# Attention and token mixer on one core: the first chunk's scores in place of dummy products, and three other moves

## The chip, the core and the metric

The kernel runs on one core of one Trainium2 chip. A core has engines that run side by side and wait for each other through semaphores: TensorE (PE in the profile, with PEld for its weight loads), VectorE (DVE), ScalarE (ACT), GpSimd (POOL) and the queue that issues transfers (SP). The metric is device time in microseconds (us): 832.36 us is the median of three runs of the kernel before (831.63 to 832.51).

## The reference

Routed attention over 4 batches, 8 heads, 768 positions and 64 dimensions, and a token and channel mixer on its output. All is float32.

```python
q_assign = argmax(q_n . c_n);  k_assign = argmax(k_n . c_n)      # 16 clusters for each head
mask   = q_assign[:, None] == k_assign[None, :]
scores = where(mask, q @ k.T / 8, -1e9)
x      = softmax(scores) @ v                                      # then (B, S, H*D) = (4, 768, 512)
h = relu(x^T @ w_tok1) @ w_tok2;   u   = x + h^T                  # token mixing
h2 = relu(u @ w_ch1) @ w_ch2;      out = u + h2                   # channel mixing
```

## The kernel before, where the change and the steps touch it

Two heads make a pair, and there are 16 pairs. Of a pair, the scores of a half of its queries (`qh`, 384 of them) against a chunk `j` of 128 keys are a tile `sc`. It is the sum of two products: one-hot cluster vectors (`ohT`, bf16; its query part carries the factor -2^33, and a key's vector holds ones at the clusters that are not its own), which adds the mask, and q and k themselves (`T`, f32). A pair has two halves of six chunks each.

```python
def scores(g, qh, beside=None):
    for j in range(NJ):                                  # NJ = 6
        if (g, qh, j) == (0, 0, 2):
            second_first()                               # one-hots of the 2nd half: turned on PE, put by DVE, counted on ACT
        sc = ps_sc.tile([P, 2, 512], F32, tag="sc", name="sc")      # 3 buffers in PSUM
        for src, start in ((st["ohT"], True), (st["T"], False)):
            for h in range(2):
                nc.tensor.matmul(sc[:, h, 0:HS], lhsT=src[rows, 1, j], rhs=src[rows, 0, js], start=start, stop=not start)
        ex = st["ex", qh, j] = work.tile([P, 2, HS], F32, name="ex")  # 9 buffers
        nc.scalar.activation(out=ex, in_=sc[:, :, 0:HS], func=ACT.Exp, scale=SM_SCALE)

def add_up(g, qh):                                       # DVE: five additions make the denominators' sums
    for j in range(1, NJ):
        nc.vector.tensor_tensor(out=acc, in0=acc if j > 1 else st["ex", qh, 0], in1=st["ex", qh, j], op=ALU.add)
```

The first pair has no earlier work to hide behind. Its beginning is written out:

```python
    keep_warm(11)                                        # dummy products of zeros
    scs = [ps_sc.tile([P, 2, 512], F32, tag="sc", name="pt") for _ in range(2)]
    tq = turn_first(0, 0, scs[0][:, 0, 0:HS])            # q of the first half turned on PE; k likewise
    ...
    keep_warm(2)
    pr = ps_sc.tile([P, 2, 512], F32, tag="sc", name="pr")
    route_products(0, pr[:, 0, 0 : HS // 2], js[0])      # similarities to the clusters, first half
    ...
    route(0, js[0])                                      # DVE: turn, maximum, one-hots
    keep_warm(3)
    route_turn_first(0)                                  # PE turns the one-hots, ACT and DVE put them into ohT
    route_products(0, pr[:, 1, 0 : HS // 2], js[1])      # second half
    route(0, js[1])
```

The loop over pairs, with what the steps need:

```python
for g in range(NPAIR):
    for qh in range(2):
        scores(g, qh, ...)
        if g == 0 and qh == 0:
            turn(1); load(2)                             # DVE turns q and k of pair 1
        if (g, qh) == (0, 1):
            route_products(1, ...); route_on(1)          # DVE: one-hots of pair 1, then a transfer that turns them
        add_up(g, qh)
    ...
    turn(g + 2); load(g + 3)
    ...
    for qh in range(2): values(g, qh)
    pair_sums(g, ...); route_products(g + 2, ...)        # both into one tile "small"
```

Token and channel mixing use Strassen's scheme in Winograd's form: seven block products (`p1 p5 c11 u2 c12 c22 c21`) and sums of blocks, `S1..S4` on the left and `T1..T4` on the right, which DVE makes. PSUM banks X, Y and Z carry the products, three buffers of X and of Z. After each product, DVE adds the bank to the result, and `between()` puts one waiting step into the stream.

```python
order = "p1 0 p1 1 p1 2 p5 0 p5 1 p5 2 c11 0 c11 1 u2 0 u2 1 u2 2 c12 0 c12 1 "
order += "c22 0 c22 1 c22 2 c12 2 c11 2 c21 0 c21 1 c21 2"
for m in ...:
    product(banks[tag, i], a, r, i, name in FIRST)       # PE
    add(x, banks[tag, i], x)                             # DVE, reads the bank
    if m in after: after[m]()
    between()                                            # late step first, then one of `others`

# second token mixing: two sums of u after product 13 (c22 0)
tok2_chunks(b, {13: lambda: (next(usums), next(usums))})

# channel mixing, first part of the first batch: the last two products of ch1 come late
def late_(i):
    product(X[i], "A22", "T4", i, False)
    nc.scalar.activation(out=a12[:, i], in_=X[i], func=ACT.Relu)
    if i == 0: sub(h2["S2"], h2["S1"], a11)
    else: sum_3(); sum_4()
late.extend([lambda: late_(0), lambda: late_(1)])
# ... and ch2_chunks starts: its p1 0, p1 1, p1 2 take the X buffers in turn
```

Of the kernel before, what the change touches and what calls it, by code (L numbers as in the profile page):

```python
# [8 lines left out]
F32 = mybir.dt.float32  # L9
BF16 = mybir.dt.bfloat16  # L10
# [7 lines left out]
B, H, S, D = 4, 8, 768, 64  # L18
C = 16
P = 128  # L20
# [30 lines left out]
def kernel(  # L51
# [320 lines left out]
    def turn_first(n, a, out):  # L372

        st = state[0]
        for j in range(HJ):
            nc.tensor.transpose(
                out=out[:, j * P : (j + 1) * P],
                in_=st["rows"][n][:, a, j].rearrange("p h d -> p (h d)"), identity=ident,
            )
        js = slice(HJ * n, HJ * n + HJ)  # L380
        return st["T"][:, a, js].rearrange("p j t -> p (j t)"), out

    def route_turn_first(n):

        for a in (1, 0):
            po = ps_av.tile([P, HJ, P], BF16, tag="av", name="po")
            for j in range(HJ):
                nc.tensor.transpose(out=po[:, j], in_=ohs[0][:, a, HJ * n + j], identity=identb)
            out = state[0]["ohT"][:, a, HJ * n : HJ * n + HJ]
            if a == 0:  # L390
                nc.vector.tensor_scalar_mul(out=out, in0=po, scalar1=-BIG)
            elif n == 0:
                nc.scalar.copy(out=out, in_=po)
            else:
                nc.vector.tensor_copy(out=out, in_=po)
# [9 lines left out]
        state[0].pop("rows")  # L405


    def scores(g, qh, beside=None):

        st = state[g]  # L410
        js = slice(HJ * qh, HJ * qh + HJ)
        for j in range(NJ):
            if (g, qh, j) == (0, 0, 2):
                second_first()
            sc = ps_sc.tile([P, 2, 512], F32, tag="sc", name="sc")
            for src, start in ((st["ohT"], True), (st["T"], False)):
                for h in range(2):
                    rows = slice(h * D, (h + 1) * D)
                    nc.tensor.matmul(  # L419
                        sc[:, h, 0:HS], lhsT=src[rows, 1, j], rhs=src[rows, 0, js],  # L420
                        start=start, stop=not start,
                    )
            if qh * NJ + j == EX and beside:
                beside()
            ex = st["ex", qh, j] = work.tile([P, 2, HS], F32, name="ex")
            nc.scalar.activation(out=ex, in_=sc[:, :, 0:HS], func=ACT.Exp, scale=SM_SCALE)  # L426

    def add_up(g, qh):
        st = state[g]
        if qh == 0:  # L430
            st["sum"] = sums.tile([P, 2, 2, HS], F32, name="sum", bufs=1)
        acc = st["sum"][:, qh]
        for j in range(1, NJ):
            nc.vector.tensor_tensor(  # L434
                out=acc, in0=acc if j > 1 else st["ex", qh, 0], in1=st["ex", qh, j], op=ALU.add
            )
# [335 lines left out]
    def ch1_pair(part, sets, beside):  # L772
# [131 lines left out]
        if sets:  # L904
            set_x("X", "Y", "p1", a12[:, 0, n0])
            sum_1()

            def late_1():
                set_x("X", None, "u2", a12[:, 0, n1])
                set_z("X", ptile("Z", HS // 2), a12)  # L910
                sub(h2["S2"], h2["S1"], a11)

            def late_2():
                set_x("X", None, "c22", a12[:, 1].rearrange("p (k t) -> p k t", k=2))
                relu(a12)
                sum_3()
                sum_4()

            late.extend([late_1, late_2])
        else:  # L920
            sum_1()
# [4 lines that stand above are left out]
                if i == 0:  # L926
                    sub(h2["S2"], h2["S1"], a11)
                else:
                    sum_3()
                    sum_4()  # L930

            late.extend([lambda: late_(0), lambda: late_(1)])

    def ch2_chunks(b, part, last, after=()):

# [57 lines left out]
    def begin():  # L993
        cen = rsmall.tile([P, D], F32, name="cen")
        nc.sync.dma_start(cen, centroids.rearrange("h c d -> (h c) d"))
        load_first()

        nc.vector.memset(ones, 1.0)
        warm = rsmall.tile([P, WMAX], BF16, name="warm")
        nc.vector.memset(warm, 0.0)  # L1000
        nc.vector.memset(cnd, 0.0)
        nc.scalar.activation(out=rsmall.tile([P, QP], F32, name="expd"), in_=ones, func=ACT.Exp)
        make_identity(nc, ident)
        nc.gpsimd.tensor_copy(out=identb, in_=ident)
        for oh in ohs:
            nc.gpsimd.memset(oh, 0.0)
        load(1)
        load_v(0)
        pw = ps_av.tile([P, HS], F32, tag="av", name="av")

        def keep_warm(n):
            for _ in range(n):
                nc.tensor.matmul(pw, lhsT=warm[:, 0:P], rhs=warm[:, P : P + HS], start=True, stop=True)

        js = [slice(0, HJ), slice(HJ, NJ)]
        keep_warm(11)
        scs = [ps_sc.tile([P, 2, 512], F32, tag="sc", name="pt") for _ in range(2)]
        tq = turn_first(0, 0, scs[0][:, 0, 0:HS])
        nc.scalar.copy(out=tq[0], in_=tq[1])
        pc = centroids_norm(cen)  # L1020
        centroids_out(pc)
        tk = turn_first(0, 1, scs[1][:, 0, 0:HS])
        nc.vector.tensor_copy(out=tk[0], in_=tk[1])
        nc.scalar.copy(out=cnT, in_=pc)
        keep_warm(2)
        pr = ps_sc.tile([P, 2, 512], F32, tag="sc", name="pr")
        route_products(0, pr[:, 0, 0 : HS // 2], js[0])
        pt = ps_sc.tile([P, 2, 512], F32, tag="sc", name="pt")
        for out, src in [turn_first(1, a, pt[:, a, 0:HS]) for a in (0, 1)]:
            nc.scalar.copy(out=out, in_=src)  # L1030
        route(0, js[0])
        keep_warm(3)
        route_turn_first(0)
        route_products(0, pr[:, 1, 0 : HS // 2], js[1])
        route(0, js[1])

    begin()
# [1 line left out]
    def route_on(g):  # L1039
        route(g)  # L1040
        route_big(g)
        route_turn(g)
# [6 lines left out]
    for g in range(NPAIR):  # L1049
        for qh in range(2):  # L1050
            scores(g, qh, g and (lambda: pair_put(g - 1)))
            if g == 0 and qh == 0:
                turn(1)
                load(2)
            if (g, qh) == (0, 1):
                route_products(1, ps_av.tile([P, HS], F32, tag="av", name="pr"))
                route_on(1)
            add_up(g, qh)
        for other in (1, 2) if g == 1 else (g + 1,) if 2 <= g < NPAIR - 1 else ():
            route_count(other)  # L1060
        if g + 2 < NPAIR:
            turn(g + 2)
        if g + 3 < NPAIR:
            load(g + 3)
        if g > 0:
            pair_out(g - 1)
        rounding(1)
        if g == NPAIR - 2:
            assert not weights
            routing.close()  # L1070
            W["ch2"] = pool("wc2pool", 1, side="right").tile([P, NCT, DM], F32, name="wc2")
            weights = list(weight_steps(stage, W, ("ch2",), 2, nc.vector))
            rounding(1)
        rounding(g == NPAIR - 1)
        for qh in range(2):
            values(g, qh)
        if g + 2 < NPAIR:
            load_v(g + 2)
        pair_turn(g)
        two = ps_sc.tile([P, 2, 512], F32, tag="sc", name="small")  # L1080
        pair_sums(g, two[:, 0, 0:HS])
        if g + 2 < NPAIR:
            route_products(g + 2, two[:, 1, 0:HS])
        pair_denominators(g)
        if g + 2 < NPAIR:
            route_on(g + 2)
        pair_reciprocals(g)
        rounding(2 if g == NPAIR - 2 else g == NPAIR - 1 or g % 2 == 0 and 0 < g < EARLY)
# [8 lines left out]
    for b in (0, 2):  # L1097
# [26 lines left out]
        if b == 2:  # L1124
            take(turning, len(turning))
            usums = u_sums()
            tok2_chunks(b, {13: lambda: (next(usums), next(usums))})
        else:
            left_weights()
            others += left_sums(0)  # L1130
            tok2_chunks(b)
            nc.sync.dma_start(spill, xs[1])
            turning = list(u_steps(0))
# [7 lines left out]
    for n, b in enumerate(batches):  # L1141
        turning = []
        for part in range(3):
            first, last = n == 0 and part == 0, n == B - 1 and part == 2
            if part == 2 and not last:
                turning = list(u_steps(batches[n + 1]))
            if first:
                others += [lambda: next(usums)] * 2
                for steps in (right_weights(0), set_left_sums(1)):
                    others += steps  # L1150
# [242 lines left out]
```

## Time and profile before

| | value |
|---|---|
| median time | 832.36 us |
| span of the profiled run | 830.0 us |
| PE busy | 818.9 us (99%) |
| DVE busy | 606.2 us (73%) |
| ACT busy | 381.3 us (46%) |
| POOL busy | 30.7 us (4%) |
| granted clock | 0.999 of full |

A row of the timeline gives the start of a group of like instructions, how long it lasted, engine, line, operation, tiles and count; what stands in brackets is the engine's idle time just before and who ended it. A float32 product shows as two records. The ends of matmuls are modelled in the profile, and so the start of the next is the better measure of what one took.

### The profile page before, as it was taken

The numbers are of one execution on the slowest core, as the hardware profiler recorded it, in microseconds if no ns is written. First come the engines' busy times: TensorE is split into PE (matmuls) and PEld (weight loads), VectorE is DVE, ScalarE is ACT, GpSimd is POOL, SyncE is SP. The second block draws the span as 40 slices with busy tenths as digits, with TensorE's granted clock in tenths as the row PEclk, the third lists the DMA queues.
The fourth block names the chain that finished last, engine by engine and source line by source line (L and its number), as shares of the span: only waits on it lengthen the run. The fifth ranks groups of instructions, "written<-read, shape, count | busy, mean of one in ns | idle before, by whom it ended". The sixth has DMA issues, their size and how long they took to land.

```text
span 830.0 us, 11458 instructions
## 1 busy us (share of the span) xinstructions
PE 818.9 (99%) x4285; PEld 525.7 (63%) x4285; DVE 606.2 (73%) x1124; ACT 381.3 (46%) x562; POOL 30.7 (4%) x28
## 2 busy tenths in 40 slices
PE   9999999999999999999999999999999999999997
PEld 4444444444444444444578787878878788787876
DVE  6879898989898878859676677655667456764654
ACT  5678777787878775145202253121541204511120
POOL 1001010101101000000000000000000000000000
PEclk9999999999999999999999999999999999999999
DMA  9886676867776334143000115000130001400002
GB/s 154 154 152 146 122 140 123 166 137 151 138 155 136 83 96 130 41 156 48 0 1 1 19 38 173 1 0 9 37 109 1 1 1 28 124 1 0 1 2 80
DMA packets 184256, 63.39 MB, mean 76 GB/s; under 512 B 172800, under 2 KB 176896, under 8 KB 183936
## 3 DMA queue, kind: packets, MB, share of 16 engines
q1 hardware_dynamic: 182592, 62.18, 34.8%
q8 instruction: 35, 0.57, 0.3%
q10 hardware_dynamic: 1600, 0.39, 0.2%
q14 instruction: 29, 0.24, 0.1%
HBM read 36.21 MB, written 7.86 MB: 53 GB/s over the span
## 4 chain that ended last, share of the span: by engine, by line
PE 90%; DVE 7%; issue 1%; ACT 0%; DMA 0%; SPq 0%; DVEq 0%; ACTq 0%
PE sc L419 18%; PE pX L940 14%; PE av L444 13%; PE pX L788 11%; PE pZ L940 7%; PE ph L523 5%; PE pY L801 4%; PE pY L940 4%; PE pZ L788 3%; PE pZ L801 3%; PE pX L762 2%; PE pX L801 2%; PE small L480 1%; DVE x L554 1%; DVE sum L434 1%; PE pZ L762 1%
## 5 line engine op out<-in xcount | busy, mean ns | idle before, releaser
L426 ACT ACTIVATE ex<-sc 128x768 f32<-128x768 f32 x192 | 151.0, 812 | 29.1 <-PE sc L419 16.9
L419 PE MATMUL sc<-qkT 64*128 64x384 f32 x768 | 155.1, 482 | 0.0
L434 DVE TENSOR_TENSOR sum<-sum,ex 128x768 f32<-128x768 f32 x128 | 127.8, 999 | 26.9 <-ACT ex L426 14.2
L444 PE MATMUL av<-ex,va 128*64 128x384 f32 x768 | 127.4, 488 | 0.0
L554 DVE TENSOR_TENSOR x<-pX,x 128x256 f32<-128x256 f32 (+1 forms) x168 | 76.1, 460 | 41.3 <-PE pX L940 40.7
L444 PEld LDWEIGHTS av<-ex,va 128*64 128x64 f32 x768 | 53.7, 137 | 71.8 <-issue 67.0
L419 PEld LDWEIGHTS sc<-qkT 64*128 64x128 f32 x768 | 67.9, 187 | 38.4 <-issue 38.3
L828 ACT COPY hA<-pX 128x384 f32<-128x384 f32 x24 | 11.5, 479 | 146.2 <-PE pX L788 146.2
L554 DVE TENSOR_TENSOR hA<-pY,hA 128x192 f32<-128x192 f32 (+1 forms) x90 | 36.8, 409 | 50.8 <-PE pY L801 36.0
L810 ACT ACTIVATE hA<-hA 128x768 f32<-128x768 f32 x35 | 29.6, 845 | 87.1 <-DVE hA L554 87.1
L788 PE MATMUL pX<-uT,wc 128*128 128x384 f32 x192 | 68.0, 487 | 0.5 <-DVE x L554 0.5
L419 PE MATMUL sc<-ohT 64*128 64x384 bf16 x384 | 62.8, 323 | 0.1
L788 PEld LDWEIGHTS pX<-uT,wc 128*128 128x128 f32 x192 | 35.7, 190 | 18.3 <-issue 1.3
L451 ACT COPY avrows<-av 128x768 uint16<-128x768 uint16 x32 | 25.5, 796 | 45.0 <-PE av L444 45.0
L554 DVE TENSOR_TENSOR x<-pZ,x 128x256 f32<-128x256 f32 (+1 forms) x84 | 36.5, 458 | 11.9 <-PE pZ L940 11.8
L523 PE MATMUL ph<-x,wt 128*128 128x512 f32 x96 | 41.6, 593 | 0.0
L419 PEld LDWEIGHTS <-ohT 64*128 64x128 bf16 x384 | 18.6, 94 | 34.3 <-issue 9.4
L940 PE MATMUL pX<-wc,hA 128*128 128x256 f32 x144 | 37.2, 381 | 1.6 <-ACT hA L925 1.2
L697 ACT COPY uT<-ucols 128x768 uint16<-128x768 uint16 x32 | 33.2, 1051 | 4.2 <-DMA ucols<-urows 4.2
L940 PE MATMUL pY<-wc,hA 128*128 128x256 f32 x144 | 35.1, 379 | 0.0
L940 PE MATMUL pZ<-wc,hS 128*128 128x256 f32 x144 | 35.0, 379 | 0.0
L788 PE MATMUL pX<-uTs,w1s 128*128 128x384 f32 x96 | 34.9, 486 | 0.0
(178 smaller groups left out, 1266.8 us busy)
## 6 DMA issues: line engine op xcount, KB each, us to landing
raw<-in_moe_w_ch_dram SPq DMA_DIRECT2D x24, 512.0 KB, 4.5
va<-in_v_dram SPq DMA_DIRECT2D x16, 384.0 KB, 3.6
out_dram<-x SPq DMA_DIRECT2D x24, 256.0 KB, 2.6
qk<-in_k_dram SPq DMA_DIRECT2D x60, 96.0 KB, 3.9
qk<-in_q_dram SPq DMA_DIRECT2D x60, 96.0 KB, 3.6
raw<-in_moe_w_tok_dram SPq DMA_DIRECT2D x3, 512.0 KB, 4.3
raw<-in_moe_w_tok_dram SPq DMA_DIRECT2D x4, 384.0 KB, 3.8
spill<-x SPq DMA_DIRECT2D x1, 1536.0 KB, 5.1
```

What stands on the lines that cost most here:

```text
L419: nc.tensor.matmul(sc[:, h, 0:HS], lhsT=src[rows, 1, j], rhs=src[rows, 0, js], start=start, stop=not start,)
L426: nc.scalar.activation(out=ex, in_=sc[:, :, 0:HS], func=ACT.Exp, scale=SM_SCALE)
L434: nc.vector.tensor_tensor(out=acc, in0=acc if j > 1 else st["ex", qh, 0], in1=st["ex", qh, j], op=ALU.add)
L444: nc.tensor.matmul(av[h * D : (h + 1) * D], lhsT=st["va"][:, h, j], rhs=ex[:, h], start=(j == 0), stop=(j == NJ - 1),)
L451: nc.scalar.copy(out=st["rows"][:, qh], in_=av.bitcast(U16).rearrange("p (t w) -> p w t", w=2))
L523: nc.tensor.matmul(pf, lhsT=W["tok1"][:, j, t * P : (t + 1) * P], rhs=xs[b][:, j], start=(j == 0), stop=(j == NJ - 1),)
L554: nc.vector.tensor_tensor(out=dst, in0=a, in1=b, op=ALU.add)
L697: nc.scalar.copy(out=out, in_=pools.pop(("ucols", i)).rearrange("p w j t -> p w (j t)"))
L788: nc.tensor.matmul(psum, lhsT=A[a][:, k, c], rhs=R[r][:, k], start=start and k == 0, stop=k == 1, skip_group_check=not start,)
L801: nc.tensor.matmul(psum, lhsT=left[which][a][:, part * P : part * P + P], rhs=right[which][r], start=start, stop=True, skip_group_check=no ...
L810: nc.scalar.activation(out=x, in_=x, func=ACT.Relu)
L940: nc.tensor.matmul(psum, lhsT=h2[a][:, k, i * P : (i + 1) * P], rhs=Bw[w][:, part + 3 * k], start=start and k == 0, stop=k == 1, skip_grou ...
```

## The change

It has four moves. None changes what is computed.

1. The q and k product of the first chunk of the first pair is issued before the one-hots are turned, in the place of three dummy products. Its tile waits open for the one-hot product. For this the buffers of the beginning are dealt out anew: q and k of the first half are turned in one tile, `pr` moves to the other PSUM pool, and one of the turned one-hots moves to the pool of the scores.
2. The turning of the second half's one-hots goes from before the third chunk to before the fourth, and the fourth chunk's product of q and k goes ahead of its one-hot product.
3. Of the first pair's second five additions, two go ahead of the routing of pair 1 on DVE.
4. Of the sums of u, the second goes from after product 13 of the second token mixing to after its last addition; and the first of the two late products of ch1 is issued at once instead of after `p1 0` of ch2.

```diff
-    def route_turn_first(n):
+    def route_turn_first(n, pq=None):
         for a in (1, 0):
-            po = ps_av.tile([P, HJ, P], BF16, tag="av", name="po")
+            po = pq if a == 0 and pq is not None else ps_av.tile([P, HJ, P], BF16, tag="av", name="po")
...
+    def score(g, sc, qh, j, name, start):
+        src = state[g][name]
+        for h in range(2):
+            rows = slice(h * D, (h + 1) * D)
+            nc.tensor.matmul(
+                sc[:, h, 0:HS], lhsT=src[rows, 1, j], rhs=src[rows, 0, HJ * qh : HJ * qh + HJ],
+                start=start, stop=not start,
+            )
+
     def scores(g, qh, beside=None):
         for j in range(NJ):
-            if (g, qh, j) == (0, 0, 2):
+            names = ["ohT", "T"]
+            if (g, qh, j) == (0, 0, HJ):
                 second_first()
-            sc = ps_sc.tile([P, 2, 512], F32, tag="sc", name="sc")
-            ... (the two products, ohT and then T)
+                names.reverse()
+            sc = st.pop("early", None)
+            if sc is None:
+                sc = ps_sc.tile([P, 2, 512], F32, tag="sc", name="sc")
+                score(g, sc, qh, j, names[0], True)
+                score(g, sc, qh, j, names[1], False)
+            else:
+                score(g, sc, qh, j, "ohT", False)
...
-    def add_up(g, qh):
+    def add_up(g, qh, js=range(1, NJ)):
...
-            late.extend([lambda: late_(0), lambda: late_(1)])
+            late_(0)
+            late.append(lambda: late_(1))
...
-        scs = [ps_sc.tile([P, 2, 512], F32, tag="sc", name="pt") for _ in range(2)]
-        tq = turn_first(0, 0, scs[0][:, 0, 0:HS])
+        turned = ps_sc.tile([P, 2, 512], F32, tag="sc", name="pt")
+        tq = turn_first(0, 0, turned[:, 0, 0:HS])
...
-        pr = ps_sc.tile([P, 2, 512], F32, tag="sc", name="pr")
-        route_products(0, pr[:, 0, 0 : HS // 2], js[0])
+        pr = ps_av.tile([P, 2, HS // 2], F32, tag="av", name="pr")
+        route_products(0, pr[:, 0], js[0])
...
-        keep_warm(3)
-        route_turn_first(0)
-        route_products(0, pr[:, 1, 0 : HS // 2], js[1])
+        pq = ps_sc.tile([P, HJ, P], BF16, tag="sc", name="po")
+        sc = state[0]["early"] = ps_sc.tile([P, 2, 512], F32, tag="sc", name="sc")
+        score(0, sc, 0, 0, "T", True)
+        route_turn_first(0, pq)
+        route_products(0, pr[:, 1], js[1])
...
             if (g, qh) == (0, 1):
                 route_products(1, ps_av.tile([P, HS], F32, tag="av", name="pr"))
+                add_up(0, 1, range(1, 3))
                 route_on(1)
-            add_up(g, qh)
+                add_up(0, 1, range(3, NJ))
+            else:
+                add_up(g, qh)
...
-            tok2_chunks(b, {13: lambda: (next(usums), next(usums))})
+            tok2_chunks(b, {13: lambda: next(usums)})
...
             if first:
+                next(usums)
                 others += [lambda: next(usums)] * 2
```

More of the change, by code (lines that the diff above doesn't have):

```diff
@@ L405, in second_first @@
         state[0].pop("rows")
+    def score(g, sc, qh, j, name, start):
[6 more added lines that the diff above has]
+            )
     def scores(g, qh, beside=None):
         st = state[g]
-        js = slice(HJ * qh, HJ * qh + HJ)
         for j in range(NJ):
-            if (g, qh, j) == (0, 0, 2):
+            names = ["ohT", "T"]
+            if (g, qh, j) == (0, 0, HJ):
                 second_first()
-            sc = ps_sc.tile([P, 2, 512], F32, tag="sc", name="sc")
[L416 to L422, printed above, removed]
+                names.reverse()
[6 more added lines that the diff above has]
+                score(g, sc, qh, j, "ohT", False)
             if qh * NJ + j == EX and beside:
@@ L426, in scores @@
             nc.scalar.activation(out=ex, in_=sc[:, :, 0:HS], func=ACT.Exp, scale=SM_SCALE)
-    def add_up(g, qh):
+    def add_up(g, qh, js=range(1, NJ)):
         st = state[g]
-        if qh == 0:
+        if "sum" not in st:
             st["sum"] = sums.tile([P, 2, 2, HS], F32, name="sum", bufs=1)
         acc = st["sum"][:, qh]
-        for j in range(1, NJ):
+        for j in js:
             nc.vector.tensor_tensor(
@@ L1021, in begin @@
         centroids_out(pc)
-        tk = turn_first(0, 1, scs[1][:, 0, 0:HS])
+        tk = turn_first(0, 1, turned[:, 1, 0:HS])
         nc.vector.tensor_copy(out=tk[0], in_=tk[1])
```

## The prediction

> **What bounds the kernel now.** I read the page first, its busy times and its chain.
>
> ```profile
> PE 818.9 (99%) x4285; PEld 525.7 (63%) x4285; DVE 606.2 (73%) x1124; ACT 381.3 (46%) x562; POOL 30.7 (4%) x28
> ...
> PE 90%; DVE 7%; issue 1%; ACT 0%; DMA 0%; SPq 0%; DVEq 0%; ACTq 0%
> ```
>
> PE is at work 99% of the span and makes 90% of the chain. So a change can win only by taking PE work away or by closing one of the few gaps on PE. The view of waits, for PE alone, lists those gaps:
>
> ```profile
> PE pX L940 <- ACT hA L925: 1.2, 2, 0.6
> PE pr L304 <- DVE qkT L1023: 0.6, 1, 0.6
> PE pX L788 <- DVE x L554: 0.5, 1, 0.5
> PE small L304 <- DVE qkT L294: 0.5, 1, 0.5
> ```
>
> Columns: total us, times, longest. These are short, since a wait counts only from the modelled end of the matmul before; measured from start to start the gaps are larger. Three of the four lines stand where the change acts, the second (the products of the first routing) does not. I then read the timeline at these places.
>
> The beginning:
>
> ```profile
> 7.84 0.65 PE L1013 MATMUL av<-warm 128*128 128x384 bf16 x3
> ...
> 8.45 0.51 PE L388 MATMUL po<-identb,oh 128*128 128x128 bf16 x6
> ```
>
> PE fills the time until the one-hots come (8.45) with three dummies, and no other PE work lies there; the first score product follows at 9.41. The end of the first pair:
>
> ```profile
> 27.86 1.83 DVE L294 STREAM_TRANSPOSE qkT<-qk 128x768 f32<-128x768 f32 x2
> ...
> 29.75 0.85 PE L304 MATMUL small<-qkT,cnd 128*32 128x384 f32 x8 [0.47 <-DVE qkT L294]
> ```
>
> PE waits for DVE to turn pair 2, so this point is set by DVE's queue and not by PE's. The end of the second token mixing:
>
> ```profile
> 389.30 0.95 DVE L551 TENSOR_TENSOR uTs<-uT 128x768 f32<-128x768 f32 x1
> ...
> 390.36 0.96 DVE L551 TENSOR_TENSOR uTs<-uT,uTs 128x768 f32<-128x768 f32 x1
> ...
> 393.63 1.88 DVE L554 TENSOR_TENSOR x<-pX,x 128x512 f32<-128x512 f32 x3
> ...
> 394.45 2.82 PE L788 MATMUL pX<-uT,wc 128*128 128x384 f32 x8 [0.50 <-DVE x L554]
> ```
>
> Two sums of u stand in DVE's queue ahead of additions that free X banks; PE's next product takes a bank only at 394.45. The first part of the channel mixing:
>
> ```profile
> 410.87 1.45 PE L788 MATMUL pX<-uTs,wc 128*128 128x384 f32 x4
> ...
> 412.36 0.49 ACT L925 ACTIVATE hA<-pX 128x384 f32<-128x384 f32 x1 [0.72 <-PE pX L788]
> ...
> 412.90 1.13 PE L940 MATMUL pX<-wc,hA 128*128 128x256 f32 x4 [0.58 <-ACT hA L925]
> ```
>
> Each late product is followed at once by a ch2 product whose X buffer is the late product's own: PE stands until ACT has read it, here and again at 415.91.
>
> **What the Trainium skill says.** "Perfetto Trace Analysis", section "Identifying the Most-Contended Engine", says that matmul busy time is a poor measure of how near PE is to its limit, because matmuls overlap. The trace agrees: a 128x512 record lasts 592 ns on average, but follows the one before after 0.43 us (six from 386.71 to 389.29). I therefore count from start to start. "PSUM — Partial Sum Buffer", section "Engine vs sequencer instructions", says that the queues of VectorE and ScalarE are strictly first in, first out, and that matmuls start and finish in program order. The trace agrees where it matters: at 393.63 DVE adds the last c21 banks after both sums of u, though u is needed later. So the order of the program is the order of the wait. "TensorEngine Tiling (Array Packing)", section "Key Properties", says that a change of the tiling mode drains TensorE. The trace shows about 0.10 us at such a place: q and k products of 64 rows repeat every 0.32 us, and the last of them before a turn (128 rows) takes 0.42.
>
> **The change part by part.**
>
> *Beginning, PE.* One chunk's q and k product is four records, two and two side by side, 2 x 0.32 = 0.64 us; the three dummies are 3 x 0.16 = 0.49, and after them PE waited 0.12. The early product starts at 7.84 and needs only what was ready at 6.5. With the 0.10 for the switch of mode, the turns start at 7.84 + 0.64 + 0.10 = 8.57 instead of 8.45: 0.12 later, and so are ohT and the first one-hot product (9.53 for 9.41). From there PE has one q and k product less, 0.64. Twelve chunks later PE is 0.64 - 0.12 = 0.52 us ahead. Moving the second turn behind the third chunk adds no work.
>
> *First pair, DVE.* Only part of this reaches the end. The first Exp can begin 0.52 earlier (9.93 for 10.45), but three now run before the counts, 9.93 + 3 x 0.81 = 12.36, and the two counts take 0.78 as before: 13.14 for 12.74. DVE's turn of pair 1 waits for them: 13.35 for 12.95, 0.40 later. Five additions follow (5.17 from 14.71 to 19.88), now until 20.28. Then the two moved additions (2.08) fill the 0.80 in which DVE waited for the routing products: until 22.36. Routing takes 2.06 (20.68 to 22.74): 24.42. Three additions of 1.04: 27.5, where it was 27.86. So pair 2 is turned 0.36 earlier and PE's product comes at 29.4 instead of 29.75. The stage wins 0.35 us, not 0.52. The turning transfer of pair 1's one-hots starts 1.5 us later and takes some 3.9 to land (28.3), ahead of the scores at 30.2.
>
> *Do the pairs after it keep this?* From pair to pair the scores begin 19.11 us apart, with almost nothing idle on PE, and where DVE holds PE once (0.27 us near 166) DVE itself was started by PE at 145.36. All of it shifts along.
>
> *Second token mixing.* With one sum of u less, c22's other additions start at 390.18, and those up to the first of c21 follow each 0.60: the bank for ch1 is free at about 393.25. PE's 16 records from 386.71 on end at 386.71 + 16 x 0.43 = 393.59. So ch1 starts at 393.59 and not 394.45: 0.86. The first record after the stand took 0.08 more, which goes too. 0.94 us. The moved sum then runs from 394.4 to 395.4; its product comes about 5 us later.
>
> *Late product.* Order now: late 0 at 410.01 (1.29), p1 0 (0.86), late 1 (1.29), p1 1 (0.86), p1 2 (0.86). Late 0's bank is read by ACT by 412.13 (after its relu of a22, until 411.64); p1 1 wants it at 413.45. Late 1's bank is read by about 414.2; p1 2 wants it at 414.31. No stand is left. p5 starts at 415.17 instead of 416.87: 1.70 us, which is two gaps of 0.74 and twice 0.10 for the first record after them. DVE has S2, S3, S4 bunched before the p1 additions, about 1.4 us behind PE; the first bank that waits for such an addition comes back five products (4.3 us) later.
>
> Sum: 0.35 + 0.94 + 1.70 = 2.99 us, and 832.36 - 2.99 = 829.4.
>
> **The rivals.** (1) DVE's new order takes the wait elsewhere: the bunched sums hold u2 or the next ch1 bank, and part of the 1.70 comes back. For it: DVE was within 0.2 us of PE in this stretch. Against it: from 421 on DVE waits 0.17 us for each product, so it catches up. If it came true, about 830.5. (2) The beginning wins nothing or loses: the early product delays the one-hots (0.12) and the counts hold DVE back more than I reckon. For it: DVE sets the end of this stage. That makes 829.8, and up to 830.2 with a loss. (3) The p1 2 bank is missed by a few hundredths, or a stand appears after the shift of other phases; 829.7. (4) All small gains vanish in a later wait: against it, the chain is PE's to the end; then 832.
>
> **Range and chances.** The repeat spread of the kernel before is 0.9 us in all. Rivals 1 to 3 all lie above my number, so the range is longer upwards: 828.5 to 831.0. Two per cent would be 16.6 us, more than all the idle time of PE: faster by over 2% 0.005, within 2% 0.985, slower 0.01.
>
> **What would show it.** In the changed profile: no wait of L940 for the late relu; the first ch1 product of the first batch about 0.9 closer to the last c21; the product of pair 2 (L304) near 29.4 and still waiting for DVE; the first scores at 9.53. PE's busy time should fall little, its gaps by some 2.5 us. I am wrong if a new wait for DVE's additions (L554) stands in ch2's first part, if that L304 comes later than 29.75, or if pairs stop being 19.11 apart.

## The result and the profile after

The changed kernel takes 829.12 us (median of 6 runs, 828.57 to 829.63). The kernel before, run beside it, takes 832.18 us (831.63 to 832.51). The ratio is 0.9965, with a 95% interval of 0.9952 to 0.9977. The span of the profiled run is 827.5 us, where it was 830.0.

The page of the changed kernel, its busy times and its chain:

```profile
PE 818.1 (99%) x4282; PEld 526.0 (64%) x4282; DVE 605.3 (73%) x1124; ACT 381.6 (46%) x562; POOL 30.6 (4%) x28
...
PE 95%; DVE 4%; ACT 0%; issue 0%; ACTq 0%; DVEq 0%
```

PE has 0.8 us less work, DVE's share of the chain has gone from 7% to 4%, and the span has 2.5 us less. So most of the gain comes from gaps and not from work. Which gaps, the view of waits of PE tells (total us, times, longest):

```profile
PE pX L952 <- ACT hA L897: 0.4, 1, 0.4
PE pt L376 <- ACT qkT L1031: 0.4, 1, 0.4
PE pX L952 <- DVE x L565: 0.2, 1, 0.2
```

Lines have moved by about twelve: the former L940, L788, L554, L925 and L551 are L952, L799, L565, L936 and L562. The late relu's wait (1.2 us in two stands) is gone, and so are ch1's wait for the additions and `small`'s wait for DVE. Of the lines shown, the first (ch2 of the last batch) and the last (ch2 near 458) are old; the middle one is new: the turning of k waits for ACT's copy of q. (Two waits in the beginning, for the dummies' zeros and of `pr`, were there before too and are left out here.)

How the 2.5 us come about, by the times of marks in both timelines (us from the start of the span):

| | before | after | what it adds to the span |
|---|---|---|---|
| k of the first half turned on PE starts | 5.27 | 6.14 | |
| first product of the first routing (`pr`) | 6.66 | 7.51 | |
| first one-hot product of the scores | 9.41 | 10.58 | |
| product of pair 2 (L304) | 29.75 | 29.90 | +0.15 |
| first product of token mixing (`ph`), after L304 | 286.48 | 286.21 | -0.27 |
| first product of ch1, after `ph` | 78.23 | 77.36 | -0.87 |
| p5 of ch2, after ch1 | 22.42 | 20.65 | -1.77 |
| from there to the last product | 406.56 | 406.56 | 0 |
| from the last product to the end | 6.55 | 6.82 | +0.27 |

The row of p5 holds 0.08 us that the prediction put to the sum of u: the first record of ch1 after a stand. The last row is the landing of the last store.

The beginning in the changed kernel's timeline (start, length, engine, line, operation, tiles, count; in brackets the idle time before and its releaser):

```profile
5.61 0.48 ACT L1031 COPY qkT<-pt 128x384 f32<-128x384 f32 x1 [1.23 <-PE pt L376]
...
6.14 0.55 PE L376 MATMUL pt<-ident,ex 128*128 128x128 f32 x3 [0.35 <-ACT qkT L1031]
...
7.51 0.53 PE L304 MATMUL pr<-qkT,cnd 128*32 128x192 f32 x8 [0.49 <-DVE qkT L1035]
...
8.78 0.92 PE L413 MATMUL sc<-qkT 64*128 64x384 f32 x4
```

The k turning begins only when ACT's copy of q has ended (5.61 + 0.48 = 6.09). Not all of the 0.87 us between 5.27 and 6.14 is the wait for this copy. The copy itself begins 0.25 later than before (5.61 for 5.36), because the turning of q ends later. x_late, a kernel of the experiments with the old beginning, also has its copy at 5.61, and it turns k at 5.53; against it the delay is 0.61. In x_late's timeline:

```profile
5.53 0.49 PE L376 MATMUL pt<-ident,ex 128*128 128x128 f32 x3
5.61 0.48 ACT L1020 COPY qkT<-pt 128x384 f32<-128x384 f32 x1 [1.23 <-PE pt L376]
```

All that follows is late, and the early product starts at 8.78 and not at 7.84. The end of the first pair, same view:

```profile
28.02 1.83 DVE L294 STREAM_TRANSPOSE qkT<-qk 128x768 f32<-128x768 f32 x2
...
29.05 0.85 PE L491 MATMUL small<-sum,ones 128*32 128x384 f32 x8
29.90 0.85 PE L304 MATMUL small<-qkT,cnd 128*32 128x384 f32 x8
```

DVE's turn ends at 29.85, and L304 starts at 29.90, straight behind the denominators' product. There is no bracket any more: PE and DVE arrive together. The end of the second token mixing:

```profile
389.30 0.95 DVE L562 TENSOR_TENSOR uTs<-uT 128x768 f32<-128x768 f32 x1
...
392.56 1.89 DVE L565 TENSOR_TENSOR x<-pX,x 128x512 f32<-128x512 f32 x3
393.47 2.75 PE L799 MATMUL pX<-uT,wc 128*128 128x384 f32 x8
394.35 0.96 DVE L562 TENSOR_TENSOR uTs<-uT,uTs 128x768 f32<-128x768 f32 x1
```

One sum stands ahead of the additions now, the other behind them, and ch1 starts without waiting. The late products:

```profile
408.95 1.45 PE L799 MATMUL pX<-uTs,wc 128*128 128x384 f32 x4
...
410.24 1.03 PE L952 MATMUL pX<-wc,hA 128*128 128x256 f32 x4
...
411.10 1.45 PE L799 MATMUL pX<-uTs,wc 128*128 128x384 f32 x4
...
412.39 1.89 PE L952 MATMUL pX<-wc,hA 128*128 128x256 f32 x8
...
414.12 2.75 PE L952 MATMUL pZ<-w2s,hS 128*128 128x256 f32 x12
```

From late 0 to p5 it is 414.12 - 408.95 = 5.17 us, and the products alone take 2 x 1.29 + 3 x 0.86 = 5.16. No gap is left.

### The profile page after: what moved, and what is told of

The parts are those of the page before. It is cut to its first block, busy times and chain, and to the rows that moved or that the text cites. A ratio compares the mean times of both kernels' runs of the same rounds, so it can differ in the third digit from the quotient of the medians.

```text
span 827.5 us, 11453 instructions
## 1 busy us (share of the span) xinstructions
PE 818.1 (99%) x4282; PEld 526.0 (64%) x4282; DVE 605.3 (73%) x1124; ACT 381.6 (46%) x562; POOL 30.6 (4%) x28
## 4 chain that ended last, share of the span: by engine, by line
PE 95%; DVE 4%; ACT 0%; issue 0%; ACTq 0%; DVEq 0%
PE sc L413 19%; PE av L455 15%; PE pX L952 14%; PE pX L799 11%; PE pZ L952 7%; PE ph L534 5%; PE pY L812 4%; PE pY L952 4%; PE pZ L799 3%; PE pZ L812 3%; PE pX L773 2%; PE pX L812 2%; PE small L491 2%; PE pZ L773 1%; PE small L304 1%; DVE hA L565 1%
## 5 line engine op out<-in xcount | busy, mean ns | idle before, releaser
L565 DVE TENSOR_TENSOR x<-pX,x 128x256 f32<-128x256 f32 (+1 forms) x168 | 76.2, 461 | 40.9 <-PE pX L952 40.4
L565 DVE TENSOR_TENSOR hA<-pY,hA 128x192 f32<-128x192 f32 (+1 forms) x90 | 36.8, 409 | 49.9 <-PE pY L812 36.0
L799 PE MATMUL pX<-uT,wc 128*128 128x384 f32 x192 | 67.9, 487 | 0.0
L799 PEld LDWEIGHTS pX<-uT,wc 128*128 128x128 f32 x192 | 35.7, 190 | 17.5 <-issue 0.6
L565 DVE TENSOR_TENSOR x<-pZ,x 128x256 f32<-128x256 f32 (+1 forms) x84 | 36.6, 459 | 11.9 <-PE pZ L952 11.8
L952 PE MATMUL pX<-wc,hA 128*128 128x256 f32 x144 | 36.9, 380 | 0.4 <-ACT hA L897 0.4
L952 PE MATMUL pY<-wc,hA 128*128 128x256 f32 x144 | 35.1, 379 | 0.0
L952 PE MATMUL pZ<-wc,hS 128*128 128x256 f32 x144 | 35.0, 379 | 0.0
L799 PE MATMUL pX<-uTs,w1s 128*128 128x384 f32 x96 | 34.9, 486 | 0.0
```

Source lines behind the costliest of these rows:

```text
L565: nc.vector.tensor_tensor(out=dst, in0=a, in1=b, op=ALU.add)
L799: nc.tensor.matmul(psum, lhsT=A[a][:, k, c], rhs=R[r][:, k], start=start and k == 0, stop=k == 1, skip_group_check=not start,)
L952: nc.tensor.matmul(psum, lhsT=h2[a][:, k, i * P : (i + 1) * P], rhs=Bw[w][:, part + 3 * k], start=start and k == 0, stop=k == 1, skip_grou ...
```

## The experiments

The theory (A in the expectations) was that the two late moves gain what the prediction said, and that the beginning gains nothing because of the shared tile for q and k. (A tile is a buffer, here in PSUM; shared means that q and k are turned into two parts of one.) The first rival was that the time at the beginning is DVE's or the load's, whatever the tiles. The second was that the new order of the early product, not the tile, makes the delay. All times are medians. The ratios are to the kernel before run beside them: 832.4 for the first three and y_twotiles, 831.97 for the others.

| run | what it is | time | ratio, 95% interval |
|---|---|---|---|
| x_late | before + late product at once | 830.86 | 0.9983, 0.9976 to 0.9990 |
| x_usum | before + later second sum of u | 831.75 | 0.9994, 0.9986 to 1.0002 |
| x_begin | before + moves 1 to 3 | 832.33 | 0.9999, 0.9991 to 1.0008 |
| y_twotiles | after + q and k in two tiles | 832.77 | 1.0001, 0.9993 to 1.0009 |
| x_shared | before + q and k in one tile | 833.05 | 1.0012, 1.0006 to 1.0019 |
| y_noadds | after without move 3 | 829.93 | 0.9975, 0.9966 to 0.9984 |
| y_bank | y_twotiles + another bank for the last denominators | 828.83 | 0.9962, 0.9949 to 0.9976 |
| z_oneload | y_bank + one register load in place of three | 828.14 | 0.9957, 0.9943 to 0.9970 |

**The late product alone.**

```diff
-            late.extend([lambda: late_(0), lambda: late_(1)])
+            late_(0)
+            late.append(lambda: late_(1))
```

> The kernel before with the early late product alone (half of move 4). Theory: both stands of 0.74 us behind the late products go, and 0.10 us twice for the first record after each; p5 of the first ch2 starts 1.70 us closer to the first ch1 product; time -1.7 us (about 830.5). Rival: DVE, with S2, S3, S4 bunched ahead of its additions, holds a bank instead, and a new wait of L940 for L554 gives back part: -0.8 us or less.

Measured: 832.4 - 830.86 = 1.5 us less; from ch1 to p5 20.73 us, which is 22.42 - 20.73 = 1.69 less. This term was sized right.

**The sum of u alone.**

```diff
-            tok2_chunks(b, {13: lambda: (next(usums), next(usums))})
+            tok2_chunks(b, {13: lambda: next(usums)})
...
             if first:
+                next(usums)
```

> The kernel before with the later second sum of u alone (the other half of move 4). Theory: the first ch1 product starts 0.86 us earlier and its first record takes 0.08 less: -0.94 us (about 831.2). Rival: the late sum T2 and the two after it come too late for u2, c22 or c21 and the wait appears there: near 0.

Measured: 831.75, 0.65 us less, with an interval that holds 1. In the trace, ch1 starts 38.79 us after the 49th record of `ph`, where it is 39.50 before: 0.71 less. In the changed kernel the same distance is 38.62, 0.88 less. The 0.17 between them comes from elsewhere: in x_usum a transfer of weights landed 0.3 us later (ACT waited 2.85 us for it, 2.55 before), DVE's additions ran late behind it, and PE lost 0.17 us from 386.89 on, where a weight load waited for such an addition. The mechanism stands; the time alone would not have shown it.

**The beginning alone.** The edit is the changed kernel with the two edits above undone.

> The kernel before with moves 1 to 3 alone. Theory A, drawn from the profile after: q and k turned in one tile make k's turn wait for ACT's copy of q, about 0.6 us, and this eats the 0.35 us that the prediction reckoned: +0.2 us (between 0 and +0.4), the turn of k in the trace ends up after the end of ACT's copy. Theory B: the late beginning of the profile after was only a late transfer, and the three moves win their 0.35 us.

Measured: 832.33 for 832.4. The k turning starts at 6.08, straight after ACT's copy of q (6.03), and L304 comes at 29.84. The interval reaches from about -0.7 to +0.7 us, so the time cannot tell a gain of 0.35 from a loss of 0.2. The trace can: in two other kernels with the old beginning, x_usum and x_late, L304 comes at 29.86 and 30.01, and here at 29.84, so the three moves at the beginning together win little or nothing there. That agrees with the theory, and it does not yet tell the shared tile from the new order.

**q and k in two tiles again, the rest of the change kept.**

```diff
-        turned = ps_sc.tile([P, 2, 512], F32, tag="sc", name="pt")
-        tq = turn_first(0, 0, turned[:, 0, 0:HS])
+        scs = [ps_sc.tile([P, 2, 512], F32, tag="sc", name="pt") for _ in range(2)]
+        tq = turn_first(0, 0, scs[0][:, 0, 0:HS])
...
-        tk = turn_first(0, 1, turned[:, 1, 0:HS])
+        tk = turn_first(0, 1, scs[1][:, 0, 0:HS])
```

> The changed kernel with q and k turned in two tiles again, as before the change; all else as changed. Theory A: the wait of k's turn for ACT's copy goes, the first routing and all behind it come some 0.6 us earlier; time -0.6 us against the changed kernel (about 828.5), unless k's transfer itself lands late. Theory B: the same time as the changed kernel.

Measured: the k turning starts at 5.59 without a wait, `pr` at 6.98, L304 at 29.38, and pair 1's scores 0.53 us sooner than in the changed kernel.

```profile
5.59 0.49 PE L376 MATMUL pt<-ident,ex 128*128 128x128 f32 x3
5.61 0.48 ACT L1031 COPY qkT<-pt 128x384 f32<-128x384 f32 x1 [1.23 <-PE pt L376]
...
29.38 0.85 PE L304 MATMUL small<-qkT,cnd 128*32 128x384 f32 x8
```

This is what the theory asks for, and the early product is still there, so the second rival falls as the cause of this wait. The time is worse all the same, 832.77 where 828.5 was expected. The timeline of this kernel where token mixing begins shows why:

```profile
317.49 0.58 DVE L495 STREAM_TRANSPOSE dent<-small 128x384 f32<-128x384 f32 x1
318.21 8.37 PE L534 MATMUL ph<-x,wt 128*128 128x512 f32 x15 [2.28 <-DVE dent L495]
```

The second tile turns the deal of the three `ps_sc` buffers by one. Now the first product of token mixing writes the bank of the last pair's `small`, which DVE reads late, behind the rounding of weights. PE stands 2.28 us. Then comes a second cost, in the table by stretches of the same kernel (stretch, length, busy time of PE, PEld, DVE, ACT, POOL, granted clock, DMA share, GB/s):

```profile
310.00:319.50 9.50, 7.22 (x43) 2.85 (x40) 8.98 (x17) 5.22 (x9) 0.00 (x0) 1.00 0.33 81
319.50:323.00 3.50, 3.50 (x6) 1.34 (x5) 3.13 (x6) 0.00 (x0) 0.00 (x0) 0.51 0.85 235
323.00:330.00 7.00, 7.00 (x18) 3.18 (x17) 1.60 (x4) 3.56 (x5) 0.00 (x0) 1.00 0.40 131
```

After the stand PE's granted clock is a half for 3.4 us (319.59 to 323.00), and PE loses half of that, 1.7 us: ch1 comes 79.02 us after `ph`, and 77.36 in the changed kernel. The Trainium skill, "TensorE: Matmul & The Clock Gate", Part 1, says that TensorE drops to half rate after an idle window of about 3.4 us. The half rate agrees with this trace. The idle time does not: PE stood 2.28 us here (2.76 from the start of the record before), and the measurement decides.

**The shared tile alone, on the kernel before.** One of two tiles less would turn the deal too, so the last pair's denominators go to `ps_av` here.

```diff
-        scs = [ps_sc.tile([P, 2, 512], F32, tag="sc", name="pt") for _ in range(2)]
-        tq = turn_first(0, 0, scs[0][:, 0, 0:HS])
+        turned = ps_sc.tile([P, 2, 512], F32, tag="sc", name="pt")
+        tq = turn_first(0, 0, turned[:, 0, 0:HS])
...
-        tk = turn_first(0, 1, scs[1][:, 0, 0:HS])
+        tk = turn_first(0, 1, turned[:, 1, 0:HS])
...
+        if g == NPAIR - 1:
+            den = ps_av.tile([P, HS], F32, tag="av", name="den")
...
```

> The kernel before with one thing of move 1 alone: q and k of the first half are turned in one tile. So that the buffers dealt out later do no harm, the last pair's sums of denominators go to the other PSUM pool. Theory A: k's turn then waits for ACT's copy of q, it starts after 6.05 us instead of 5.3 to 5.5, the first routing some 0.55 us later, and all behind it: +0.5 us. Theory B: the shared tile costs nothing, time as before.

Measured: 833.05 for 831.97, 1.1 us more. The waits of PE in this kernel:

```profile
PE small L304 <- DVE qkT L294: 0.9, 1, 0.9
...
PE pt L376 <- ACT qkT L1019: 0.4, 1, 0.4
```

The wait for ACT's copy of q comes with the shared tile, and nothing else of the change is in this kernel. The fair comparison is x_late, which has the old beginning and whose copy of q starts at the same 5.61: k's turn comes at 6.14 for 5.53 and `pr` at 7.54 for 6.92, 0.62 late. L304 comes at 31.05 for 30.01, 1.04 late. The other 0.42 is not the tile's: it is a pause of DVE between two like additions, which this kernel has here and the kernel before has not.

```profile
24.68 3.08 DVE L434 TENSOR_TENSOR sum<-sum,ex 128x768 f32<-128x768 f32 x3
...
28.28 0.96 DVE L434 TENSOR_TENSOR sum<-sum,ex 128x768 f32<-128x768 f32 x1 [0.52 <-DVE sum L434]
```

The kernel before has such a pause later, near 159, and this one does not (see the last section), so 0.27 comes back there: `ph` follows L304 after 286.21 us and not 286.48. The tile alone costs 0.6 us of the 1.1, much the same as the 0.5 to 0.6 that two tiles win in the changed kernel. The first rival holds for a smaller part: of the 0.88 us by which `pr` is later than in the kernel before (7.54 for 6.66), 0.26 stands in x_late too.

**Move 3 undone.**

```diff
-                add_up(0, 1, range(1, 3))
                 route_on(1)
-                add_up(0, 1, range(3, NJ))
-            else:
-                add_up(g, qh)
+            add_up(g, qh)
```

> The changed kernel without move 3: all five additions of the second half stand behind the routing of pair 1. From the working of the prediction: DVE is busy until PE's routing products come anyway, so nothing changes (0). From the trace after: DVE would idle 0.2 us at 21.0 and end later; L304 of pair 2 at 30.3 for 29.9, +0.4 us. Rival: move 3 made the whole gain of the stage; L304 waits for DVE by 0.8 us or more.

The end of the first pair in this kernel's timeline:

```profile
28.40 1.83 DVE L294 STREAM_TRANSPOSE qkT<-qk 128x768 f32<-128x768 f32 x2
...
30.28 0.85 PE L304 MATMUL small<-qkT,cnd 128*32 128x384 f32 x8 [0.46 <-DVE qkT L294]
```

DVE turns pair 2 at 28.40 where the changed kernel has 28.02, and L304 is 0.38 later and waits again (0.46, counted from k's turn, which began 0.08 earlier here). Move 3 is worth about 0.4 us there. The time is 829.93: the ratio is 0.9975 where the changed kernel has 0.9965, and the two intervals overlap. Of the difference, 0.27 us is the pause of DVE near 159, which this kernel has and the changed one has not (`ph` 286.48 after L304).

**Two tiles without the bank's wait.** y_twotiles, with the last pair's denominators in `ps_av`:

```diff
-        two = ps_sc.tile([P, 2, 512], F32, tag="sc", name="small")
-        pair_sums(g, two[:, 0, 0:HS])
+        if g == NPAIR - 1:
+            den = ps_av.tile([P, HS], F32, tag="av", name="den")
+        else:
+            two = ps_sc.tile([P, 2, 512], F32, tag="sc", name="small")
+            den = two[:, 0, 0:HS]
+        pair_sums(g, den)
```

> The changed kernel with two tiles for turning q and k, and the last pair's sums of denominators in the other PSUM pool, so that the first product of the token mixing takes no bank that DVE still has to read. Theory A: the 2.3 us wait of y_twotiles in front of L534 goes, and with it the drop of the clock behind it; the beginning keeps its 0.5 us; -0.5 us against the changed kernel, about 828.6. Rival: the wait there was DVE's lateness and stays in another form, and the time stays near that of y_twotiles, 832.

Measured: 828.83 (828.60 to 829.05). The k turning starts at 5.53, L304 at 29.33, and `ph` at 315.80 without a wait; the granted clock is 0.998. So the stand in y_twotiles was the bank's, and the half clock came with the stand. At L304 this kernel is 0.58 us ahead of the changed one, at `ph` only 0.31, because the distance between them is 286.48 here and 286.21 there (see the last section).

**One register load.** The last of PE's waits late in the kernel stands where ch2 of the last batch begins, and the profile puts it down to an ACT copy (L897). By that point PE's own queue also loads three counts into registers. This kernel is y_bank with the three counts summed by DVE first:

```diff
-        nc.vector.tensor_copy(out=count, in_=pn)
+        total = const.tile([1, 1], F32, name="total")
+        nc.vector.reduce_sum(out=total, in_=pn, axis=AX.X)
+        nc.vector.tensor_copy(out=count[:, 0:1], in_=total)
...
-        loaded = [
-            nc.values_load(count[0:1, i : i + 1], min_val=0, max_val=P) for i in range(3)
-        ]
-        return loaded[0] + loaded[1] + loaded[2]
+        return nc.values_load(count[0:1, 0:1], min_val=0, max_val=3 * P)
```

> As y_bank, and the three counts that every engine loads into registers ahead of the last ch2 are added up on DVE first, so that each engine loads one value instead of three. In the traces PE stands 0.63 us at that place (L952 behind L812, put down to ACT). Theory: the stand is the loads' own time, and a third of them leaves about 0.2: -0.4 us against y_bank, about 828.2. Rival: the stand is ACT's copy, as the profile says: no change against y_bank.

The place in the changed kernel's timeline (y_bank has the same wait of 0.40):

```profile
800.83 0.49 PE L812 MATMUL pY<-uTs,wc 128*128 128x192 f32 x2
801.07 0.46 ACT L897 COPY hA<-pX 128x384 f32<-128x384 f32 x1
...
801.72 1.10 PE L952 MATMUL pX<-wc,hA 128*128 128x256 f32 x4 [0.40 <-ACT hA L897]
```

and in this kernel's:

```profile
800.37 0.49 PE L812 MATMUL pY<-uTs,wc 128*128 128x192 f32 x2
800.61 0.46 ACT L897 COPY hA<-pX 128x384 f32<-128x384 f32 x1
800.70 1.03 PE L952 MATMUL pX<-wc,hA 128*128 128x256 f32 x4
```

L952 follows L812 after 0.33 us where it took 0.89, and PE starts while the copy that it was said to wait for is still running (until 801.07). So it was not waiting for ACT: the loads held it. From p5 to the last product it is 405.98 us for 406.56, and the time is 828.14 (828.09 to 828.60), the shortest of all the kernels here. Two loads fewer closed 0.56 us here, 0.28 for each (an estimate, half of the 0.56).

## Why the prediction was right, and where it was not

The time was predicted as 829.4 and is 829.12. Part of this closeness is luck: the two late gains are as reckoned, but the beginning won nothing, and a pause of DVE that the prediction did not know of went away and made that good.

1. *Late product, 1.70.* Right: 1.69 alone (x_late), and 1.69 in the changed kernel (22.42 - 20.65, less the 0.08 of ch1's first record). All waits named for it are gone.
2. *Second token mixing, 0.94.* Right: the changed kernel's ch1 comes 0.87 nearer to `ph`, and with the first record it is 0.95. x_usum by itself showed 0.71, because a late transfer took 0.17 of it. The order ran as predicted: a sum, the additions, ch1 at 393.47, then the second sum at 394.35.
3. *Beginning and first pair, 0.35.* Wrong. The step that failed is "The early product starts at 7.84 and needs only what was ready at 6.5". The diff turns q and k in one tile, and I had listed this as a new deal of buffers and given it no cost. With one tile, k's turning waits until ACT has read q, so the product starts at 8.78 and the first scores at 10.58, not at 9.53. L304 comes at 29.90, where 29.4 was predicted and 29.75 was before; later than 29.75 was one of the prediction's own signs of being wrong. (The mark is not firm: x_late, with the old beginning, has 30.01.) With two tiles L304 comes at 29.38, 29.33 and 29.19, so the shared tile, 0.5 to 0.6 us, eats what the three moves win.

   That two tiles give the predicted 29.4 is luck in its turn, for two errors cancel in it. From k's turn to the first one-hot product it takes 4.14 us before and 4.46 in y_twotiles: the early product costs 0.32 and not 0.12. With k's turn 0.31 later than in the kernel before, the first Exp comes at 10.43 and not at 9.93. From there to L304 the prediction's times give 19.47 (29.4 - 9.93), and it takes 18.95. Rival 2 described the outcome (nothing won), and the part of its cause that it put at 0.12 is real; the shared tile was not in it.
4. *Move 3.* In the prediction the two additions fill time in which DVE waits, and by its sums pair 2 is turned at 27.5 with them or without. With the late scores they are worth about 0.4 us (y_noadds), which is why the changed kernel loses only 0.15 at L304.
5. *"All of it shifts along".* Wrong by 0.27, in the lucky direction. The pairs stay 19.11 apart, but the hold of PE near 166 is gone from the changed kernel, and it makes good what the beginning lost: +0.15 and -0.27 in place of -0.35. It was put down to PE, which had started DVE at 145.36; the traces show a pause of DVE itself (last section).
6. *Rivals 1, 3 and 4.* None came: no new wait for L565 in ch2's first part, no stand at p1 2, and both late gains reach the end.

The profiled span fell by 2.5 us and the medians by 3.1; the 0.27 at the tail lies in the landing of one store. The spread of the repeats (about 1 us) leaves the remaining difference open. The times of x_late, x_usum and x_begin add up to a gain of 2.3 us only; that spread leaves this open too.

## What to carry to other kernels

When a change deals buffers anew, read each tile that two writers now share as a new wait, and count through the pool who gets which buffer afterwards: one tile more at the start cost a 2.3 us stand 310 us later. A gain of under 1 us is better read between two marks of the trace than from the time, one move at a time, and both marks should lie behind the first transfers: k's turn begins anywhere from 5.27 to 5.59 in kernels with two tiles. And a wait that the profile gives to another engine may be the engine's own queue; take away that other thing and see whether PE starts before the named releaser ends.

## What the runs showed of the hardware

**Half clock after a stand of 2.3 us.** In y_twotiles, as shown above: 3.4 us at half clock, about 1.7 us lost, on top of the stand. It begins 1.4 us after PE is back at work (319.59 for 318.21). y_bank, without the stand, has none.

**A pause of DVE that comes with the program.** The hold near 166 goes back to a pause of 0.42 us (idle 0.48, of which 0.06 is usual) between two like additions. In the timeline of the kernel before:

```profile
156.50 2.02 DVE L434 TENSOR_TENSOR sum<-sum,ex 128x768 f32<-128x768 f32 x2
159.00 2.02 DVE L434 TENSOR_TENSOR sum<-sum,ex 128x768 f32<-128x768 f32 x2 [0.48 <-DVE sum L434]
```

and the same four additions in the changed kernel:

```profile
156.65 4.15 DVE L445 TENSOR_TENSOR sum<-sum,ex 128x768 f32<-128x768 f32 x4
```

It is there in x_late, x_usum and y_noadds behind the same addition and in y_bank one addition later, and it is absent in x_begin and x_shared. With it, `ph` comes 286.48 us after L304, without it 286.21. Kernels with the same stream of DVE agree in it, so it goes with the program and not with the run. In all these traces it stands before the 320th instruction recorded on DVE; the pause of x_shared at 28.28 stands before the 64th, 256 earlier. That points to a place given by the count of instructions and not by the work, but no run here shows this, nor the cause of the pause; it stays open.
